# A fused attention and mixture-of-experts kernel on one core: last output tile in two halves, output stores of one batch reordered, and new order tables for all engines

## Chip, cores and metric

The kernel runs on one core of a Trainium2 chip. The metric is the device time in microseconds (us) of one execution; three runs of a kernel give a median. TensorE (PE) does the matmuls, VectorE (DVE), ScalarE (ACT) and GpSimd (POOL) the elementwise work, and SyncE (SP) only issues DMA transfers in this kernel.

## What is computed

Three stages in a row, all in 32-bit floats. Attention with a mask: every query and key goes to the nearest of 16 centroids, and a query sees only the keys of its own cluster. Its output, 1536 tokens of 512, goes through a layer `ln(solu(x @ w_in)) @ w_out` with 1024 inner columns, and then through `((x @ w_a) * (x @ w_b)) @ w_out` with 1536.

```python
q_assign = np.argmax(np.einsum('bhsd,hcd->bhsc', q_n, c_n), axis=-1)
mask = q_assign[:, :, :, None] == k_assign[:, :, None, :]
scores = np.where(mask, scale * np.matmul(q, k.transpose(0, 1, 3, 2)), -1000000000.0)
...
h = x @ w_in
solu = h * softmax(h)
x = (layernorm(solu) * g_ln) @ w_out
...
return (x @ w_a) * (x @ w_b) @ w_out
```

Shapes: 2 batches, 8 heads, 768 positions of 64; the output is two batches of 768 rows of 512 floats, twelve tiles of 128 rows and 256 KB.

## The kernel before

**A plan and order tables.** The program is first laid out as a list of operations. `Plan.add` (L245) takes one: its engine, a cost, a rank, and the buffers it reads and writes. Operations are numbered in the order in which they are added, and these numbers stand in the text below. `Plan.schedule` (L299) walks `SEQ` (from L37), one table of operation numbers for each engine, written into the file; each engine's instructions are issued strictly in the order of its table. What an operation depends on is worked out from its buffers, and an engine that comes to an operation whose inputs are not there waits, with all that stands behind it. The tables hold 840 entries for PE, 942 for DVE, 711 for ACT, 302 for POOL and 233 for SP. An operation can be several instructions: 12 matmuls, say.

**All transfers on one queue.** `dma` (L495) issues every DMA on SP, in the order of SP's table. A transfer whose source is not ready holds up those behind it.

**Precision by splitting.** A product of 32-bit floats is made of three matmuls of a rounded "hi" and a remainder "lo". So a weight or an activation takes an ACT cast (hi) and a subtraction on DVE (L485) or POOL (L483) for lo.

**The attention stage**, up to about 400 us, goes over eight pairs of heads. `do_load` (L669) loads q, k and v of a pair, 384 KB each. `qk_part` (L742) transposes and splits q and k; POOL's L758 and L760 make operands that `do_place` (L817) then copies from SBUF to SBUF into the layout that the scores need. `do_oh` (L922, ACT's L927) and `do_ohd` (L929) make the one-hot cluster rows and put them beside q and k, in transfers of 24 KB, four for each half of a pair. `score` (L1005) then has the score matmuls (L1014), the max (DVE L1018) and the exponential (ACT L1022); `turn` (L1030) transposes it (PE L1046, copies on ACT L1055 and DVE L1053); `apply` multiplies by v (PE L1070), merges halves (ACT L1083, DVE L1084) and normalises. Beside it run the weights of the next stage: `load_win` (L572) loads w_in and rounds and splits it with integer operations (DVE L579, POOL L595).

**The middle stage** is `moe_h`, `moe_ln`, `moe_x2` and `x_pack` (casts at L1294), up to about 400 us as well. **The last stage** works in 12 units; each has `quartet` (matmuls L1384, evacuations on ACT L1359, additions on DVE L1363 and L1369, hi on ACT L1373, lo on DVE L485) and then `moe2_y`, which multiplies a unit's 768 rows (six tiles of 128) by w_out (L1441). Two sums of a tile run in PSUM over the visits of a batch and are added on DVE (L1457) to a buffer in SBUF; after the last visit of a batch each tile's store to the output is issued (L1460). Batch 1 ends with unit 10, batch 0 with unit 11, the last. In unit 11 a tile gets three matmuls for each of two w_out blocks, 512 columns each. Tiles 0 and 1 are in the PSUM pair psS0, tiles 2 and 3 in psS1, tile 4 in psO, tile 5 in psM; psT0 and psT1 hold the quartet's results.

In this kernel tile 4 of unit 11 is added and stored in two halves of 256 columns, and the others whole; tile 0 is the last. SP's table ends with batch 1's six stores in the order of tiles 4, 2, 5, 3, 0, 1, and then batch 0's: 3, 5, 1, the halves of 4, 2, 0.

Of the kernel before, what the change touches and what calls it, by code (L numbers as in the profile page):

```python
# [83 lines left out]
    ),  # L84
    "DVE": (
# [287 lines left out]
def dve(n):  # L373
    return n / 0.96 + 69
# [1162 lines left out]
```

## Time and profile before

| | |
|---|---|
| median of 3 runs | 680.87 us (680.80 to 681.03) |
| profiled execution | 681.25 us |
| its span | 679.4 us |
| PE, DVE, ACT, POOL busy | 99%, 77%, 57%, 42% of the span |
| DMA | 58.49 MB moved, mean 86 GB/s |

The profile has one execution. Busy time is what instructions of an engine lasted; "idle before" is what an engine waited ahead of an instruction, with the engine or DMA that let it go. PE's weight loads (PEld) are recorded apart from its matmuls and overlap them. SPq is SP's queue of DMA issues. [...]

### The profile page before, as it was taken

To read this page: it belongs to the slowest core of one execution; us is meant where nothing else is said; L and a number is where in the kernel's file an instruction comes from. 1 tells how busy PE (TensorE), PEld (TensorE's weight loads), DVE (VectorE), ACT (ScalarE), POOL (GpSimd) and SP (SyncE) were. 2 spreads that over 40 slices of the span, in tenths; PEclk is the share of its full clock that TensorE was granted. 3 is DMA by queue.
4 is the path that set the end of the run, shared out by engine and by line. 5 is a ranking of instruction groups with operands and counts; after the bars stand their busy time and mean duration, and the time that the engine had idled before them with its cause. 6 is when DMAs were issued, how large, how long until landed. Compare 5 with 4: busy or idle time off the path is not lost.

```text
span 679.4 us, 10935 instructions
## 1 busy us (share of the span) xinstructions
PE 671.3 (99%) x3910; PEld 576.0 (85%) x3910; DVE 523.1 (77%) x943; ACT 389.4 (57%) x820; POOL 285.8 (42%) x323
## 2 busy tenths in 40 slices
PE   8999999999999999999999999999999999999997
PEld 7777777777777767888999999998989999989996
DVE  6978797798778878999869359796876757977436
ACT  5877777768677864574464555554654543534221
POOL 4024554635456433244445477644335432542000
PEclk9999999999999999999999999999999999999999
DMA  4367447473722612110211002132112212110005
GB/s 140 97 157 192 115 119 189 121 169 83 203 85 71 161 38 63 32 62 32 66 59 62 1 1 91 65 116 72 62 63 94 93 63 63 63 62 32 1 0 187
DMA packets 33094, 58.49 MB, mean 86 GB/s; under 512 B 3848, under 2 KB 21904, under 8 KB 33040
## 3 DMA queue, kind: packets, MB, share of 16 engines
q1 hardware_dynamic: 33040, 57.79, 30.0%
q8 instruction: 31, 0.51, 0.3%
q14 instruction: 23, 0.19, 0.1%
HBM read 36.74 MB, written 3.15 MB: 59 GB/s over the span
## 4 chain that ended last, share of the span: by engine, by line
PE 93%; DVE 4%; ACT 1%; DMA 1%; issue 1%; SPq 0%; DVEq 0%; ACTq 0%
PE psT L1384 25%; PE psS L1162 10%; PE psO L1070 10%; PE psS L1441 9%; PE psS L1014 9%; PE psT L1046 9%; PE psO L1254 5%; PE psM L1254 5%; PE psO L1441 2%; PE psM L1441 2%; PE psT L1237 2%; PE psM L750 1%; PE psM L841 1%; PE psM L1099 1%; PE psM L845 1%; DMA R<-R 1%
## 5 line engine op out<-in xcount | busy, mean ns | idle before, releaser
L1384 PE MATMUL psT<-R 128*128 128x384 f32 x1008 | 181.8, 336 | 0.4 <-DVE F L1363 0.3
L1384 PEld LDWEIGHTS psT<-R 128*128 128x128 f32 x1008 | 175.8, 188 | 4.8 <-ACT F L1359 1.3
L483 POOL TENSOR_TENSOR R<-F,R 128x256 fp32r<-128x256 f32 (+3 forms) x92 | 109.7, 1202 | 98.0 <-ACT R L1294 51.5
L595 POOL TENSOR_TENSOR F<-F 128x512 int32<-128x512 int32 x45 | 60.8, 1350 | 110.3 <-DVE F L591 96.3
L1359 ACT COPY F<-psT 128x384 f32<-128x384 f32 x108 | 51.5, 480 | 91.9 <-PE psT L1384 84.8
L1022 ACT ACTIVATE F<-psS,mxn 128x768 f32<-128x768 f32 x96 | 86.7, 905 | 23.2 <-DVE mxn L1018 16.7
L1018 DVE TENSOR_REDUCE mxn<-psS 128x1 f32<-128x768 f32 x96 | 90.4, 951 | 10.6 <-PE psS L1014 9.4
L1014 PE MATMUL psS<-R 128*128 128x512 f32 (+3 forms) x384 | 89.9, 358 | 0.9 <-DMA R<-R 0.6
L1046 PE MATMUL psT<-ident,F 128*128 128x128 f32 x576 | 85.8, 275 | 0.2
L1046 PEld LDWEIGHTS psT<-ident,F 128*128 128x128 f32 x576 | 65.4, 140 | 13.3 <-ACT F L1022 6.3
L1014 PEld LDWEIGHTS psS<-R 128*128 128x128 f32 (+1 forms) x384 | 65.6, 190 | 12.2 <-ACT F L1022 2.6
L1441 PE MATMUL psS<-R 128*128 128x512 f32 x288 | 74.9, 391 | 0.0
L1162 PE MATMUL psS<-R 128*128 128x512 f32 x288 | 69.3, 394 | 0.0
L1070 PE MATMUL psO<-F 128*64 128x384 f32 x384 | 69.0, 494 | 0.0
L1053 DVE COPY F<-psT 128x384 f32<-128x384 f32 x96 | 52.8, 550 | 15.5 <-PE psT L1046 14.2
L1441 PEld LDWEIGHTS psS<-R 128*128 128x128 f32 x288 | 53.8, 188 | 10.3
L1162 PEld LDWEIGHTS psS<-R 128*128 128x128 f32 x288 | 53.0, 188 | 10.5
L485 DVE TENSOR_TENSOR R<-F,R 128x384 fp32r<-128x384 f32 (+1 forms) x72 | 53.3, 753 | 8.5 <-ACT R L1373 3.9
L1363 DVE TENSOR_TENSOR F<-psT,F 128x384 f32<-128x384 f32 x48 | 26.7, 555 | 39.8 <-PE psT L1384 35.0
L1055 ACT COPY F<-psT 128x384 f32<-128x384 f32 x96 | 45.9, 479 | 19.7 <-PE psT L1046 18.3
L1369 DVE TENSOR_TENSOR F<-F 128x384 f32<-128x384 f32 x60 | 44.3, 742 | 10.6 <-ACT F L1359 10.1
L1070 PEld LDWEIGHTS psO<-F 128*64 128x64 f32 x384 | 24.7, 136 | 28.2 <-issue 26.6
(158 smaller groups left out, 1000.2 us busy)
## 6 DMA issues: line engine op xcount, KB each, us to landing
F<-in_moe_w_out_dram SPq DMA_DIRECT2D x20, 512.0 KB, 3.3
R<-R SPq DMA_DIRECT2D x28, 288.0 KB, 4.4
F<-in_moe_w_a_dram SPq DMA_DIRECT2D x12, 512.0 KB, 3.7
F<-in_moe_w_b_dram SPq DMA_DIRECT2D x12, 512.0 KB, 3.6
R<-R SPq DMA_DIRECT2D x28, 192.0 KB, 3.9
F<-in_moe_w_in_dram SPq DMA_DIRECT2D x8, 512.0 KB, 4.9
F<-in_v_dram SPq DMA_DIRECT2D x8, 384.0 KB, 5.1
out_dram<-F SPq DMA_DIRECT2D x11, 256.0 KB, 2.6
```

The source lines that it names most:

```text
L483: pl.add("POOL", pool(n), rank, lambda: G.tensor_tensor(out=out_, in0=in0, in1=in1, op=ALU.subtract), reads, writes)
L485: pl.add("DVE", dve(n), rank, lambda: V.tensor_tensor(out=out_, in0=in0, in1=in1, op=ALU.subtract), reads, writes, port=port)
L595: pl.add("POOL", pool(n), rank, lambda: G.tensor_tensor(out=ui, in0=ui, in1=low, op=ALU.add), [rk, lwk], [uk])
L1014: T.matmul(sp[:, c0:c0 + cn], kq[:r, 2 * m, t * P:(t + 1) * P], kq[:r, 2 * m + 1, c0:c0 + cn], start=m == 0, stop=m == 1)
L1018: pl.add("DVE", dve(S), i + SUB["max"], lambda: V.tensor_reduce(out=mxn[:, b:b + 1], in_=sp[:, :S], axis=AX.X, op=ALU.max, negate=True), [ ...
L1022: pl.add("ACT", act(S) + 93 + 93, i + SUB["exp"], lambda: A.activation(F[:, po:po + 768], sp[:, :S], AF.Exp, bias=mxn[:, b:b + 1], scale=1 ...
L1046: T.transpose(sp[:, c, :], pt[:, kt * P:(kt + 1) * P], ident)
L1070: T.matmul(psO[rs, :AN], vs[:, j, kt % HT * 2 + kt // HT], pt[:, kt, :], start=kt < 2, stop=kt >= NT - 2, tile_position=(0, kt % 2 * D), s ...
L1162: T.matmul(sp[:, n0:n0 + 512], xv5[:, i, a, c], winv[:, w, c, n0:n0 + 512], start=first, stop=(c == KD - 1 and a == 1))
L1254: T.matmul(sp[:, :GN], wo1v(f, w)[:, ds_], d[a][:, f, :], start=(f == 0 and x == 0), stop=(f == NF1 - 1 and x == 2))
L1384: T.matmul(t[:, :AN], wv[l][0][:, c], xp_[:, a, xi, c], start=(x in (0, 1, 3) and c == 0 and l == 0 and a == 0), stop=(c == 1 and l == 1), ...
L1441: T.matmul(yt, hy(j, a)[0][:, gg * P:(gg + 1) * P], R[:, wo + l * 512:wo + (l + 1) * 512], start=(u in first_u and fl == 0 and a == 0 and ...
```

## The change

Four things. First, all the order tables are replaced: 302 entries of PE's, 631 of DVE's, 432 of ACT's, 194 of POOL's and 178 of SP's stand at another place. Second, tile 0 of the last unit is taken out of `moe2_y` and done by a new function, `last_y`: two halves of 256 columns, in psT0 and psT1, each with all six matmuls (both w_out blocks), one addition and one store of 128 KB. All of it stands at the end of the tables. Third, tile 4's addition and store in two halves become one of each. Fourth, batch 1's stores stand on SP in the order of tiles 3, 5, 2, 4, 1, 0, which is the order in which DVE's table has their additions; batch 0's are 3, 5, 4, 1, 2 and the halves of 0.

The table entries that the prediction speaks of: 42, the v load of the first pair of heads; 142 and 141, place DMAs behind POOL's L758; 740 to 743 and 744 to 747, the one-hot DMAs of the first and the second half of pair 4; 732 and 701, place DMAs; 692, a v load; 713 and 317, w_in loads; 966, a rounding of w_in on DVE (L579); 1363, a merge on ACT (L1083); 1942, a cast on ACT (L1294); 2264, a subtraction on DVE (L485); 908, the k load of pair 6; 872, a v load; 929, a one-hot DMA.

```diff
     "SP": (
-        39, 7, 38, 107, 40, 41, 137, 187, 108, 42, 8, 142, 138, 139, 109, 158, 156, 165, 163, 166, 186, 164,
...
+        39, 7, 38, 40, 107, 41, 187, 138, 108, 8, 186, 142, 141, 42, 140, 139, 317, 153, 165, 163, 154, 158,
...
-        702, 732, 701, 692, 735, 688, 704, 731, 742, 740, 736, 700, 733, 713, 744, 743, 747, 746, 741, 918, 897,
...
+        703, 587, 734, 733, 704, 736, 705, 688, 732, 740, 741, 743, 742, 746, 692, 701, 747, 713, 744, 918, 897,
...
+        895, 916, 894, 896, 921, 917, 840, 919, 745, 899, 920, 898, 909, 923, 922, 925, 924, 929, 872, 908, 965,
...
-        2708, 2702, 2747, 2761, 2816, 2810, 2899, 2976, 2973, 2967, 2964, 2970, 2961, 3014, 3017, 3011, 3026,
-        3028, 3023, 3020,
...
+        2708, 2702, 2747, 2761, 2810, 2816, 2899, 2964, 2967, 2973, 2976, 2961, 2970, 3013, 3016, 3028, 3010,
+        3025, 3022, 3019,
     ),
...
+    def last_y(u, b):
+
+        o = ACC_[b * NT]
+        rk = T1 + (u + 2) * U
+        fj = [(fl, j) for j, (fl, half_) in enumerate(YO) if half_ == 0]
...
+        for x in range(2):
+            yt, yk, cs = psT[x][:, :DM // 2], f"psT{x}", slice(x * DM // 2, (x + 1) * DM // 2)
+            av, fk = F[:, o + cs.start:o + cs.stop], fc((o + cs.start, DM // 2))
+
+            def mm(yt=yt, cs=cs):
+                for fl, j in fj:
+                    for a, l in ((0, 0), (0, 1), (1, 0)):
+                        c0 = w0[fl] + l * 512 + cs.start
+                        T.matmul(yt, hy(j, a)[0][:, :P], R[:, c0:c0 + DM // 2], start=(fl == 0 and a == 0 and l == 0), stop=(fl == 1 and a == 1))
+
+            pl.add("PE", mm_cost(DM // 2, 6), rk + x * 0.6, mm, [*hk, *[rc((w, 1024)) for w in w0]], [yk])
+            pl.add("DVE", dve(DM // 2), rk + x * 0.6 + 0.1, lambda av=av, yt=yt: V.tensor_tensor(out=av, in0=yt, in1=av, op=ALU.add), [yk], [fk])
+            dma(128, rk + x * 0.6, lambda av=av, cs=cs: Y.dma_start(outv[b, 0, 0, :, cs], av), [fk], [])
...
+            if u == NU - 1 and t == 0:
+                if fl:
+                    last_y(u, b)
+                continue
...
-                m = 2 if u == NU - 1 and j == 3 and gg == 2 else 1
-                for x in range(m):
-                    cs = slice(x * DM // m, (x + 1) * DM // m)
-                    fk = fc((o + cs.start, DM // m))
-                    pl.add("DVE", dve(512 // m), rk + 0.1, lambda av=av[:, cs], yt=yt[:, cs]: V.tensor_tensor(
-                        out=av, in0=yt, in1=av, op=ALU.add), [yk], [fk])
-                    if not left[u]:
-                        dma(256 // m, rk, lambda av=av[:, cs], t=t, cs=cs: Y.dma_start(outv[b, t // HT, t % HT, :, cs], av), [fk], [])
+                fk = fc((o, 512))
+                pl.add("DVE", dve(512), rk + 0.1, lambda av=av, yt=yt: V.tensor_tensor(out=av, in0=yt, in1=av, op=ALU.add), [yk], [fk])
+                if not left[u]:
+                    dma(256, rk, lambda av=av, t=t: Y.dma_start(outv[b, t // HT, t % HT], av), [fk], [])
```

## Rows read from the trace of the kernel before

**Rows 1.** The page's chain of work that ended last: shares by engine.

```profile
PE 93%; DVE 4%; ACT 1%; DMA 1%; issue 1%; SPq 0%; DVEq 0%; ACTq 0%
```

**Rows 2.** Windows: length, busy PE, PEld, DVE, ACT, POOL, clock, DMA share, GB/s.

```profile
0.00:17.00 17.00, 14.56 (x91) 11.93 (x92) 11.86 (x31) 9.64 (x22) 7.77 (x35) 1.00 0.45 140
17.00:660.00 643.00, 641.33 (x3749) 550.95 (x3748) 500.09 (x894) 376.52 (x791) 278.05 (x288) 1.00 0.30 82
660.00:679.40 19.40, 15.38 (x74) 13.08 (x72) 11.18 (x20) 3.29 (x7) 0.00 (x0) 0.96 0.44 163
```

**Rows 3.** Timeline of the tail: start us, us, engine, line, what, count [idle before].

```profile
667.00 9.47 SPq L1460 DMA_DIRECT2D out_dram<-F  x13
...
673.86 1.52 PE L1441 MATMUL psS<-R 128*128 128x512 f32 x6
...
674.74 1.37 DVE L1457 TENSOR_TENSOR F<-psS,F 128x512 f32<-128x512 f32 x2
```

**Rows 4.** SP's last issue; DMA issues at 676.1 and 674.9: KB, us to landing.

```profile
676.14 0.33 SPq L1460 DMA_DIRECT2D out_dram<-F  x1
...
out_dram<-F SPq DMA_DIRECT2D x1, 256.0 KB, 2.0
...
out_dram<-F SPq DMA_DIRECT2D x1, 128.0 KB, 1.8
```

**Rows 5.** Groups by line and form: count | busy us, mean ns | idle before.

```profile
L1441 PE MATMUL psS<-R 128*128 128x512 f32 x288 | 74.9, 391 | 0.0
...
L1441 PEld LDWEIGHTS psS<-R 128*128 128x128 f32 x288 | 53.8, 188 | 10.3
...
L1014 PE MATMUL psS<-R 128*128 128x256 f32 x96 | 27.2, 283 | 0.0
...
L1457 DVE TENSOR_TENSOR F<-psO,F 128x256 f32<-128x256 f32 x2 | 0.8, 420 | 0.7 <-PE psO L1441 0.7
```

**Rows 6.** Timeline of PE in the opening.

```profile
8.79 0.83 PE L810 MATMUL psM<-cb,R 128*128 128x64 f32 x6
```

**Rows 7.** Timeline of PE near 133 us, and of SP from 123 us.

```profile
133.46 0.74 PE L1014 MATMUL psS<-R 80*128 80x512 f32 x3 [0.58 <-DMA R<-R]
...
123.31 1.20 SPq L934 DMA_DIRECT2D R<-R  x2
...
128.09 3.40 SPq L934 DMA_DIRECT2D R<-R  x5
```

**Rows 8.** Timeline of DVE and PE near 462 us.

```profile
460.06 2.23 DVE L485 TENSOR_TENSOR R<-F,R 128x384 fp32r<-128x384 f32 x2
462.21 0.54 DVE L1363 TENSOR_TENSOR F<-psT,F 128x384 f32<-128x384 f32 x1
...
462.81 0.62 PE L1384 MATMUL psT<-R 128*128 128x384 f32 x2 [0.25 <-DVE F L1363]
```

**Rows 9.** Timeline of PE's weight loads at three small waits.

```profile
179.80 0.31 PEld L1046 LDWEIGHTS psT<-ident,F 128*128 128x128 f32 x3 [0.80 <-ACT F L1022]
...
233.85 0.31 PEld L1046 LDWEIGHTS psT<-ident,F 128*128 128x128 f32 x3 [0.23 <-ACT F L1055]
...
402.88 0.47 PEld L1384 LDWEIGHTS psT<-R 128*128 128x128 f32 x3 [0.31 <-ACT F L1359]
```

**Rows 10.** DMA issues at 23.9 and 148 us; timeline of POOL, ACT and PE.

```profile
F<-in_v_dram SPq DMA_DIRECT2D x1, 384.0 KB, 5.5
...
F<-in_k_dram SPq DMA_DIRECT2D x1, 384.0 KB, 7.8
...
21.42 0.51 POOL L758 TENSOR_SCALAR R<-F 128x384 fp32r<-128x384 f32 x1 [6.56 <-ACT F L757]
...
27.80 2.16 PE L1070 MATMUL psO<-F 128*64 128x384 f32 x12
...
162.56 0.48 ACT L927 CAST R<-psM 128x384 fp32r<-128x384 bf16 x1
...
169.02 0.49 PE L750 MATMUL psM<-ident,F 128*128 128x128 f32 x3
```

More of the change, by code (lines that the diff above doesn't have):

```diff
@@ L1428, in tile_cluster_attention_moe_moe2 @@
     left = {us[-1]: sum(1 for b2, v in visits[i + 1:] if b2 == b) for i, (b, us) in enumerate(visits)}
+    def last_y(u, b):
+        o = ACC_[b * NT]
+        rk = T1 + (u + 2) * U
+        fj = [(fl, j) for j, (fl, half_) in enumerate(YO) if half_ == 0]
+        hk = [rc((HY_ + j * 2 * AN, P), (HY_ + (j * 2 + 1) * AN, P)) for fl, j in fj]
+        w0 = [WY_[(u // 2 * 2 + fl) % 3] for fl in range(2)]
+        for x in range(2):
[9 more added lines that the diff above has]
+            dma(128, rk + x * 0.6, lambda av=av, cs=cs: Y.dma_start(outv[b, 0, 0, :, cs], av), [fk], [])
     def moe2_y(u, j):
```

315 rows, old and new, of the table SEQ are left out of this document.

## Prediction, made before the change was run

> **What bounds the kernel now.** I read four views: the chain of work that ended last (who is on it), the windows (where TensorE, PE, is idle), the timeline round each idle place (what it waited for), and the DMA issues of the same moments. The chain is PE for 93%, VectorE (DVE) for 4% [rows 1]. In three windows PE is busy 14.56 of 17, 641.33 of 643 and 15.38 of 19.4 us [rows 2]. The reader is to see three places where time can be saved: the opening, some 1.7 us of idle in the long middle, and the tail, where 4 us pass after the last matmul. The middle's idle understates what a wait costs: matmuls are pipelined, a 512-column one lasts 391 ns while six take 1.52 [rows 3, 5], so they start every (1.52 − 0.39)/5 = 0.226 us; a matmul that comes late loses the shown idle plus that overlap, 0.391 − 0.226 = 0.16. Sums are made against the profiled execution, 681.25 us with a span of 679.4; the median is 680.87, and I carry the difference over to it.
>
> **Tail: the last tile in two halves.** Now the last three matmuls of tile 0 end at 673.86 + 1.52 = 675.38, a 512-column addition of 1.37/2 = 0.69 follows, and the last store is issued at 676.14 [rows 3, 4]. It is 256 KB and lands after 2.0; a 128 KB store nearby took 1.8 [rows 4]. After the change the last addition has 256 columns, 0.42 each now [rows 5]: −0.27. The last store has 128 KB: −0.2. PE pays for it. A 256-column matmul lasts 283, a 512-column one 391 [rows 5], so columns cost 108 ns per 256, and 256-column ones should start every 0.226 − 0.108 = 0.118 us: twelve take 1.42 where six took 6 × 0.226 = 1.36: +0.06. The weight loads double in number (12 for 6) and run beside the matmuls. Three of tile 0's six old matmuls came early, and now all twelve stand at the end; that moves other tiles' matmuls earlier by the same time and costs nothing by itself. Tail: −0.27 − 0.2 + 0.06 = about **−0.4**; bounds −0.55 and +0.43. The upper one is for weight loads that set the pace, 188 ns each in L1441 [rows 5]: 12 × 0.188 − 1.36 = +0.90 for PE, so −0.27 − 0.2 + 0.90. I take the lower price because six L810 matmuls of 64 columns, each with a load of its own, take 0.83 together [rows 6], so one in at most 0.14; the rest of their price is in the range.
>
> The trace lets the halves start about twice as often as the wholes. [...]
>
> **Order of batch 1's stores, and tile 4's two halves made whole.** The 13 stores leave from 667.00 on, after waiting for tile 4's addition, all while PE has work to 675.38 [rows 3]. The last one follows its addition within 0.03 us (676.11 to 676.14) [rows 3, 4], so SP's queue had drained. Sending the first six earlier gains nothing: **0**, and up to +0.2 if it brings more traffic under batch 0's. Tile 4's single addition of 0.69 for 0.84 in two parts: 0, hidden by PE.
>
> **Tables, 133 us.** PE's score matmul waited, idle 0.58, for an SBUF-to-SBUF DMA [rows 7]: the one-hot rows 741 and 743 of pair 4's first half. On SP they stand behind w_in load 713 and among the five of the row at 128.09, after the second half's 744; each such issue takes 1.20/2 = 0.6 [rows 7]. The change puts 740, 741, 743, 742 together, directly behind 732 and ahead of 713, 744, 746 and 747, so they leave from about 123.3 and land, even after 4 us, before 128.3, five before they are read. What is passed over (713, 746, 747, 692 and 701) has no reader as near. What is late next is PE itself. 0.58 plus an overlap of 0.16 to 0.24: **−0.8**.
>
> **462 us.** PE's idle of 0.25 waits for DVE's L1363 [rows 8]: it began at 462.21, behind two L485 subtractions (460.06, 2.23 us), though the matmuls it reads were done before. In the new DVE table 2264 (one of these, 1.1) and a 0.55 operation go behind L1363, three of 0.41 to 0.43 come ahead: about −0.45, so the wait is gone: 0.25 + 0.16 = **−0.4**. The moved subtraction ends later; its reader is on PE some microseconds on.
>
> **Three small ones.** PE's weight load for the transposes at 179.80 waits 0.80 for an exponential [rows 9], that one for a max reduction, and that stood behind a DVE w_in operation (966), which goes behind it; PE's matmuls themselves start about 0.2 late: −0.2. At 233.85 PE waits for an ACT copy that stood behind L1083's (1363), 0.23 for the weight load; at 402.88 its weight load waits 0.31 for an evacuation that stood behind a cast (1942) [rows 9]. Both go behind: −0.2 and −0.25. A move of one engine's operation past another issues nothing else; none of these has a DMA. Together **−0.65**.
>
> **The opening** is reordered on DVE and ACT too. I find no wait that it surely removes: **0**, bounds −0.15 and +0.15.
>
> **What the new order can spoil.** Some thousand entries change place, POOL's among them, and a wait it makes is in no row of this trace. I bound it by nothing and by the middle's whole present idle, 1.67 [rows 2], and take **+0.5**, a third of that, since the moves that I followed mostly leave PE's order as it was.
>
> The sum: −0.4 + 0 − 0.8 − 0.4 − 0.65 + 0 + 0.5 = −1.75, that is 679.5 for the profiled execution and **679.1** beside the median. The terms' ends give 677.9 (tail −0.55, opening −0.15, no new wait, half a microsecond of idle gone that I didn't trace) to 679.6 (new waits of 1.0).
>
> **Rivals.** *Waits change place.* The one-hot DMA, the subtraction and the cast that moved back now come late elsewhere, as many as were removed, and only the tail's gain stays: 680.87 − 0.4 = 680.4, with 680.9 where the tail gives nothing either. For it: PE is already 99.7% busy in the middle [rows 2], so any operation on another engine that comes 0.2 late shows. Against: the 133 us wait is the largest and its DMAs get some five microseconds of room.
>
> *Halves dear on PE.* If starts and not columns set the pace, twelve halves cost up to 0.9 more than six wholes, since a weight load lasts 188 ns [rows 5]; half of that is 0.45. The tail is then 0 to +0.43, and with the rest kept the time is 679.5 to 679.9. For it: the last matmuls run with nothing else beside them. Against: the L810 row, where loads overlap. [...]
>
> *Slower: big loads put back too far.* On SP the first v load (384 KB, before issued at 13.59) goes behind two place DMAs that wait for POOL's L758, over at 21.42 + 0.51 [rows 10]: two issues later, about 23.2, it leaves (behind it on SP wait two more place DMAs and w_in load 317, with later readers), and PE first reads it at 27.80 (about 28.9 after, where two more PE operations stand ahead). The k load 908 goes behind a one-hot DMA that waits for ACT's L927 (162.56; about 162.0 after) and a v load: 163.3, and PE's L750 needs it at 169.02 [rows 10]. A v load at about that time took 5.5, the slowest 384 KB load 7.8 [rows 10]. It decides where a load takes over 5.7. At 5.5 both are in time, the first by 0.2 only; at 7.8 the first is 23.2 + 7.8 − 28.9 = 2.1 late, the second 163.3 + 7.8 − 169.0 = 2.1: +4.2 − 1.75, so 683.3. Against it: the 7.8 came with far more DMA work queued than stands before either.
>
> **Chances.** Forecast 0.57; waits change place 0.27; halves dear 0.07; slower 0.09. A measurement of this kernel can tell about 0.2% (1.36 us) from no change, so faster is below 679.51 and slower above 682.23. The forecast's range 677.9 to 679.6 lies nearly all below the first bound; halves dear is split. Faster 0.59, same 0.32, slower 0.09. The range takes in the forecast and nearly all of the second case, and leaves out the slower one and some 0.1 more: 677.9 to 680.8.
>
> **What would show it.** In the new trace: a last L1457 addition of 256 columns (0.42) followed by a 128 KB store landing in 1.8, and the end some 4 − 0.47 = 3.6 after the last matmul; twelve last matmuls in about 1.4 us; no wait of L1014 on a DMA near 133; no L1363 wait near 462; the idle of 17 to 660 below 1.0. I am wrong if that idle is as large as before at other places (second case), if PE's last twelve matmuls take over 1.8 (third), or if L1070 near 28 or L750 near 169 waits for a DMA of v or k (fourth).

## The result: slower by 0.7%

| | before | after |
|---|---|---|
| median | 680.97 us (6 runs) | 685.90 us (6 runs) |
| ratio | | 1.0067 (95% interval 1.0054 to 1.0080) |
| span of the profiled execution | 679.4 us | 684.2 us |

The forecast was 679.1, range 677.9 to 680.8. The tail and the wait at 133 us came out about as priced. The loss lies where the prediction had put a zero, in the opening; in new waits, whose sum it had taken too low; and in small moves whose gain did not last. The windows of the kernel after, with the columns of [rows 2]:

```profile
0.00:17.00 17.00, 13.14 (x79) 9.92 (x79) 11.67 (x27) 8.79 (x19) 7.65 (x35) 0.94 0.42 121
17.00:660.00 643.00, 640.64 (x3735) 550.15 (x3735) 502.12 (x891) 376.48 (x793) 276.51 (x288) 1.00 0.30 83
660.00:684.20 24.20, 21.02 (x105) 18.28 (x103) 14.21 (x25) 4.16 (x9) 0.00 (x0) 0.99 0.36 131
...
14.00:16.00 2.00, 0.66 (x4) 0.50 (x4) 1.97 (x4) 0.10 (x1) 1.07 (x2) 0.74 0.89 275
16.00:18.00 2.00, 2.00 (x8) 1.30 (x9) 0.84 (x2) 1.26 (x3) 0.00 (x0) 0.50 0.89 292
18.00:20.00 2.00, 2.00 (x9) 1.81 (x9) 1.05 (x3) 0.25 (x2) 0.00 (x0) 0.50 0.20 67
20.00:22.00 2.00, 2.00 (x8) 1.93 (x8) 1.58 (x3) 0.27 (x1) 0.00 (x0) 0.56 0.00 0
22.00:24.00 2.00, 1.66 (x11) 1.27 (x11) 1.51 (x3) 1.62 (x4) 0.00 (x0) 1.00 0.00 0
```

Look at the column after POOL's, PE's granted clock as a share of the full one. In before it is 1.00 in both windows up to 660 us; here it falls to 0.50 between 16 and 20 us. PE is busy only 0.66 of the 2 us from 14 to 16. After that it is busy all the time, yet with only 8 or 9 matmuls in 2 us: the six of L810 take 1.32 at 17.57, where in before they take 0.75 at 15.35. The window from 17 to 660 has 643.00 - 640.64 = 2.36 us of idle PE, where the prediction wanted to see less than 1.0.

To find where the rest went I set the start of the n-th PE operation of the kernel after against the n-th of before. The difference is -0.1 at 10 us, +4.0 at 18, +3.8 at 35 (0.24 won back by a better order of two transposes and an exponential), +4.0 at 120, +3.0 at 140 (the wait at 133 is gone: -0.85 from 130 on), +3.2 at 310, +4.4 at 340, +4.7 at 410, +5.9 at 430 and +5.6 at 670; after the last matmul it falls to +4.8. Each kernel has one trace; that such differences also move by some tenths between two executions is an estimate, from the times of the kernel before, 680.6 to 683.3 us.

**The opening.** Timeline near 13 us, first of the kernel before (two lines), then of the kernel after:

```profile
12.93 0.59 DVE L888 TENSOR_TENSOR F<-F,mx 128x192 bf16<-128x192 f32 x1
13.57 0.35 PE L905 MATMUL psM<-F 128*64 128x128 bf16 x3
...
12.65 0.50 POOL L793 TENSOR_SCALAR R<-R 64x384 fp32r<-64x384 f32 x1
12.78 2.50 DVE L888 TENSOR_TENSOR F<-F,mx 128x192 bf16<-128x192 f32 x1
13.12 1.94 POOL L760 TENSOR_TENSOR R<-F,R 128x384 fp32r<-128x384 f32 x2
...
15.34 0.53 PE L905 MATMUL psM<-F 128*64 128x128 bf16 x3 [1.39 <-DVE F L888]
```

In the kernel after, DVE's L888 begins while POOL works and ends at 15.28, just after POOL's third operation in a row (13.12 + 1.94 = 15.06). At 25.12, with POOL idle, the same operation takes 0.35. PE waits 1.39 for it, and then its clock is at 0.50.

**The new waits in the middle** look alike. At 425 and at 309, DVE beside POOL:

```profile
425.03 1.31 POOL L595 TENSOR_TENSOR F<-F 128x512 int32<-128x512 int32 x1 [1.50 <-DVE F L591]
425.05 1.71 DVE L1369 TENSOR_TENSOR F<-F 128x384 f32<-128x384 f32 x1 [0.17 <-ACT F L1359]
426.68 0.54 DVE L1363 TENSOR_TENSOR F<-psT,F 128x384 f32<-128x384 f32 x1
427.28 0.97 PE L1384 MATMUL psT<-R 128*128 128x384 f32 x4 [0.70 <-DVE F L1363]
...
308.98 1.31 DVE L1199 SCALAR_TENSOR_TENSOR stt<-stt 128x1 f32<-128x1 f32 x1
...
309.00 1.28 POOL L483 TENSOR_TENSOR R<-F,R 128x512 fp32r<-128x512 f32 x1 [0.73 <-ACT R L612]
```

An L1369 takes 0.55 alone and an L1199 0.22. Here neither ends before the POOL operation beside it: L1199 ends with it (310.29 and 310.28), L1369 0.42 later (426.76 and 426.34). Below, a DVE operation that takes longer beside a running POOL operation than without one is called held.

**The tail** is as the prediction had it. Timeline of the end, to be read against [rows 3, 4]:

```profile
679.43 1.59 PE L1445 MATMUL psT<-R 128*128 128x256 f32 x12
680.34 0.42 DVE L1448 TENSOR_TENSOR F<-psT,F 128x256 f32<-128x256 f32 x1
680.80 1.05 SPq L1449 DMA_DIRECT2D out_dram<-F  x2
681.06 0.42 DVE L1448 TENSOR_TENSOR F<-psT,F 128x256 f32<-128x256 f32 x1 [0.29 <-PE psT L1445]
```

The last matmul ends at 679.43 + 1.59 = 681.02 and the span at 684.17: 3.15 where before had 4.04. Of this gain of 0.89, 0.30 lies behind the landing of the last store and isn't the new tail's (see the end).

### The profile page after: what moved, and what is told of

It is laid out like the page before. It is cut to its first block, busy times and chain, and to the rows that moved or that the text cites. A ratio compares the mean times of both kernels' runs of the same rounds, so it can differ in the third digit from the quotient of the medians.

```text
span 684.2 us, 10970 instructions
## 1 busy us (share of the span) xinstructions
PE 674.8 (99%) x3916; PEld 578.4 (85%) x3916; DVE 528.0 (77%) x943; ACT 389.4 (57%) x820; POOL 284.2 (42%) x323
## 3 DMA queue, kind: packets, MB, share of 16 engines
HBM read 36.74 MB, written 3.15 MB: 58 GB/s over the span
## 4 chain that ended last, share of the span: by engine, by line
PE 91%; DVE 6%; ACT 1%; issue 1%; DMA 0%; POOL 0%; DVEq 0%; ACTq 0%
PE psT L1384 24%; PE psS L1014 10%; PE psT L1046 9%; PE psO L1070 9%; PE psS L1466 9%; PE psS L1162 8%; PE psM L1254 5%; PE psO L1254 5%; PE psO L1466 2%; PE psM L1466 2%; PE psM L841 2%; PE psT L1237 1%; PE psM L750 1%; DVE F L1369 1%; PE psM L1099 1%
## 5 line engine op out<-in xcount | busy, mean ns | idle before, releaser
L483 POOL TENSOR_TENSOR R<-F,R 128x512 fp32r<-128x512 f32 (+3 forms) x92 | 109.2, 1196 | 110.0 <-ACT R L1294 58.6
L595 POOL TENSOR_TENSOR F<-F 128x512 int32<-128x512 int32 x45 | 61.2, 1363 | 100.4 <-DVE F L591 90.5
L1022 ACT ACTIVATE F<-psS,mxn 128x768 f32<-128x768 f32 x96 | 86.7, 904 | 23.9 <-DVE mxn L1018 17.4
L1070 PE MATMUL psO<-F 128*64 128x384 f32 x384 | 69.0, 495 | 0.0
L485 DVE TENSOR_TENSOR R<-F,R 128x384 fp32r<-128x384 f32 (+1 forms) x72 | 57.1, 810 | 11.6 <-ACT R L1373 6.7
L1363 DVE TENSOR_TENSOR F<-psT,F 128x384 f32<-128x384 f32 x48 | 26.6, 555 | 36.6 <-PE psT L1384 27.1
L1369 DVE TENSOR_TENSOR F<-F 128x384 f32<-128x384 f32 x60 | 41.9, 708 | 10.4 <-ACT F L1359 10.0
L1070 PEld LDWEIGHTS psO<-F 128*64 128x64 f32 x384 | 24.7, 136 | 28.2 <-issue 26.5
```

What stands on the lines that cost most here:

```text
L483: pl.add("POOL", pool(n), rank, lambda: G.tensor_tensor(out=out_, in0=in0, in1=in1, op=ALU.subtract), reads, writes)
L485: pl.add("DVE", dve(n), rank, lambda: V.tensor_tensor(out=out_, in0=in0, in1=in1, op=ALU.subtract), reads, writes, port=port)
L595: pl.add("POOL", pool(n), rank, lambda: G.tensor_tensor(out=ui, in0=ui, in1=low, op=ALU.add), [rk, lwk], [uk])
L1022: pl.add("ACT", act(S) + 93 + 93, i + SUB["exp"], lambda: A.activation(F[:, po:po + 768], sp[:, :S], AF.Exp, bias=mxn[:, b:b + 1], scale=1 ...
L1070: T.matmul(psO[rs, :AN], vs[:, j, kt % HT * 2 + kt // HT], pt[:, kt, :], start=kt < 2, stop=kt >= NT - 2, tile_position=(0, kt % 2 * D), s ...
```

## Experiments

In the comparisons below the kernel before ran beside each on the same chip and took 681.4 to 681.7 us, so ratios are compared. All but the run with work added for PE and those with the new tail change entries of the tables alone.

**POOL's opening put back.**

```diff
     "POOL": (
-        2, 6, 0, 10, 4, 77, 5, 45, 81, 112, 116, 49, 117, 113, 132, 133,
+        2, 6, 4, 0, 10, 5, 49, 77, 112, 81, 113, 116, 117, 45, 132, 133,
```

> The kernel after, with the first 14 entries of POOL's table in the order of the kernel before; nothing else. Theory P (three POOL operations run back to back at 12.65 to 15.06, DVE's L888 is held beside them for 2.5 us instead of about 0.6, PE waits 1.4 for it and its granted clock falls to the lower level until 22): L888 lasts 0.6 or less, no low clock in 14 to 22, time 685.9 - 4.0 = 681.9, give or take 0.4. Theory W (the warm-up matmuls that moved on PE let the clock fall): the clock still falls, 685 to 686. Theory S (the many new waits later make it slower): 685.5 or more.

Measured: ratio 1.0002 (0.9992 to 1.0011), 681.92 us; the clock is 1.00 throughout. Timeline of this run:

```profile
12.71 0.51 POOL L758 TENSOR_SCALAR R<-F 128x384 fp32r<-128x384 f32 x1
12.83 0.60 DVE L888 TENSOR_TENSOR F<-F,mx 128x192 bf16<-128x192 f32 x1
13.30 1.01 POOL L760 TENSOR_TENSOR R<-F,R 128x384 fp32r<-128x384 f32 x1
13.46 0.90 DVE L890 TENSOR_SCALAR F<-F 128x96 bf16<-128x96 bf16 x1
13.92 0.36 PE L905 MATMUL psM<-F 128*64 128x128 bf16 x3
```

POOL pauses between 13.22 and 13.30, and L888 takes 0.60 and not 2.50: it ends at 13.43. Fourteen entries of POOL's table hold nearly the whole loss. With them put back the change is neither faster nor slower than before: the forecast's 1.75 us is still missing.

**POOL's opening of after in the kernel before.**

```diff
     "POOL": (
-        2, 6, 4, 0, 10, 5, 49, 77, 112, 81, 113, 116, 117, 45, 132, 133,
+        2, 6, 0, 10, 4, 77, 5, 45, 81, 112, 116, 49, 117, 113, 132, 133,
```

> The kernel before, with the first 14 entries of POOL's table in the order of the kernel after; nothing else. Theory P: L888 lasts about 2.5, PE waits about 1.4 near 14 us and the clock falls: 681.0 + 4.0 = 685.0. Theories W and S: no change, 680.8 to 681.3.

Measured: 686.27 us, ratio 1.0073 (1.0058 to 1.0088). The timeline and the clock of two windows:

```profile
12.98 2.49 DVE L888 TENSOR_TENSOR F<-F,mx 128x192 bf16<-128x192 f32 x1
13.32 1.94 POOL L760 TENSOR_TENSOR R<-F,R 128x384 fp32r<-128x384 f32 x2
15.53 0.49 PE L905 MATMUL psM<-F 128*64 128x128 bf16 x3 [1.93 <-DVE F L888]
...
16.00:18.00 2.00, 2.00 (x7) 1.30 (x7) 0.88 (x3) 0.76 (x2) 0.00 (x0) 0.50 0.99 368
18.00:20.00 2.00, 2.00 (x9) 1.80 (x9) 0.78 (x2) 0.75 (x3) 0.00 (x0) 0.50 0.04 9
```

So POOL's order alone is enough, in either direction.

**The wait kept, PE given work in it.** The kernel after with

```diff
-            pl.add("PE", 227, 1e6 + 100 + x, lambda: T.matmul(psS[1][:, :512], cb[:, :P], cb[:, :512], start=True, stop=True), ["cb"], ["psS1"], release=WARM[0])
+            pl.add("PE", 227, 1e6 + 100 + x, lambda x=x: [T.matmul(psS[1][:, :512], cb[:, :P], cb[:, :512], start=True, stop=True) for _ in range(7 if x == 5 else 1)], ["cb"], ["psS1"], release=WARM[0])
```

> The kernel after, in which the sixth warm-up operation issues seven matmuls instead of one, so that PE has 1.4 us of work while it waits for L888 (the added matmuls write a PSUM bank that nobody reads). If most of the loss is the lower clock and not the wait itself: L888 still lasts 2.5, the clock stays at its upper level, 685.9 - 2.5 = 683.4. If the wait itself is the loss: 685.5 to 686.

Measured: 684.01 us, ratio 1.0035 (1.0023 to 1.0046).

```profile
12.92 2.52 DVE L888 TENSOR_TENSOR F<-F,mx 128x192 bf16<-128x192 f32 x1
13.37 2.07 PE L732 MATMUL psS<-cb 128*128 128x512 f32 x8
15.49 0.35 PE L905 MATMUL psM<-F 128*64 128x128 bf16 x3
...
14.00:16.00 2.00, 1.95 (x11) 1.23 (x9) 1.97 (x3) 0.12 (x1) 1.22 (x2) 1.00 0.76 255
16.00:18.00 2.00, 2.00 (x13) 1.48 (x13) 1.45 (x4) 1.49 (x4) 0.00 (x0) 1.00 0.89 272
```

L888 is as long as ever (2.52), yet with PE given work beside it the clock stays at 1.00, where in the kernel after, with PE idle for 1.39, it is at 0.50. By the ratios the fall costs 1.0067 - 1.0035 = 0.0032 of 681.6, or 2.2 us. By the n-th PE operation, the added ones left out, this run stands at +1.6 at 18 us and the kernel after at +4.0: 2.4 for the clock there, and 1.6 for the late L888 itself. I had expected 2.5 for the clock.

**PE's order round the warm-up matmuls, in the kernel before.**

```diff
     "PE": (
-        121, 122, 87, 91, 72, 123, 69, 124, 125,
+        121, 87, 91, 122, 123, 72, 124, 69, 125,
```

> The kernel before, with only the nine PE entries round the warm-up matmuls (121 to 125) in the order of the kernel after. Theory P: within 0.4 of 681.0, the clock stays up. Theory W: the clock falls near 14 us, 683.5 to 685.

Measured: ratio 1.0004 (0.9994 to 1.0013), clock 1.00. The moved warm-up matmuls are not the cause.

**The one-hot DMAs alone, in the kernel before.**

```diff
     "SP": (
-        742, 740, 736, 700, 733, 713, 744, 743, 747, 746, 741,
+        742, 740, 743, 741, 736, 700, 733, 713, 744, 747, 746,
```

> The kernel before, with only two SP entries moved: the one-hot DMAs 741 and 743 directly behind 740. Theory (the wait at 133 us is what the queue order cost, 0.58 idle plus overlap): no wait on a DMA near 133, ratio to before 0.9988 (-0.8 us). Rival (the wait takes another place, as the sum's forecast rival had it): ratio 1.0000.

Measured: ratio 0.9987 (0.9978 to 0.9995), -0.9 us. Timelines of PE and SP:

```profile
133.00 0.97 PE L1014 MATMUL psS<-R 128*128 128x512 f32 x4
...
123.93 2.46 SPq L934 DMA_DIRECT2D R<-R  x4
```

The four one-hot DMAs leave together at 123.93 and the score matmuls run through [rows 7]. Against before the PE starts step forward by 0.85 at 133 us (+0.62 to -0.23) and keep that to the end: this gain is not given back.

**The tail alone, in the kernel before**: `last_y` and its entries, all other entries in the old order (the numbers of the last tiles' operations shift with the new function).

```diff
     "PE": (
-        3004, 3008, 3007, 3003, 3012, 3006, 3015, 3009, 3005, 3024, 3021, 3018,
+        3003, 3007, 3006, 3011, 3005, 3014, 3008, 3004, 3026, 3023, 3020, 3017,
```

> The kernel before, with only the tail changed: tile 0 of the last unit in two halves of 256 columns, tile 4 whole, all else in the order of before (the stores of batch 1 too). Theory: -0.4 to -0.8 us, ratio 0.999, the twelve last matmuls in about 1.4 us. Rival (starts and not columns set the pace of 256-column matmuls): twelve last matmuls 1.8 to 2.3 us, ratio 1.000 to 1.0006.

Measured: ratio 0.9998 (0.9989 to 1.0006), which tells neither. Its trace does: the same twelve matmuls in 1.59, as in the kernel after, so they start every (1.59 - 0.28)/11 = 0.119 us, and from the last matmul to the end 3.60 instead of 4.04. The rival of dear halves is out. A likely reason why the time shows so little of it is in the section on the hardware.

**Batch 1's store order alone, in the kernel before.**

```diff
     "SP": (
-        2899, 2976, 2973, 2967, 2964, 2970, 2961,
+        2899, 2964, 2967, 2973, 2976, 2961, 2970,
```

> The kernel before, with only batch 1's six stores in the new order on SP (tiles 3, 5, 2, 4, 1, 0). Theory (they lie under PE's work and SP's queue has drained before the last store): ratio 1.0000, the last store issued 0.03 us after its addition as before. Rival (later batch 1 stores collide with batch 0's, or the earlier start clears the way): 0.2 to 0.4 us either way, ratio 0.9995 or 1.0005.

Measured: ratio 1.0006 (0.9997 to 1.0015), no difference that can be told. From the last matmul to the end its trace has 4.04, as before.

**The priced moves and nothing else, in the kernel before**: tail, one-hot DMAs, and

```diff
 ACT:  1942 behind 2067;  1363 behind 1357
 DVE:  966 behind 1042;  2264, 2194, 2272, 2190  ->  2264, 2190, 2272, 2194
```

> The kernel before with the moves that the prediction priced and nothing else: tail, one-hot DMAs, ACT's 1942 behind 2067 and 1363 behind 1357, DVE's 966 behind 1042, and near 462 DVE's 2190 and 2272 ahead of 2194. If the priced terms are right and the loss lies in what the full tables add: -0.4 -0.8 -0.25 -0.2 -0.2 -0.4 = -2.25 to -2.6, ratio 0.9964. If each removed wait is given back: ratio 0.999 to 1.000.

Measured: ratio 0.9989 (0.9980 to 0.9998), no more than the one-hot DMAs alone. Timeline at two of the moves:

```profile
179.37 0.55 PE L1046 MATMUL psT<-ident,F 128*128 128x128 f32 x3
...
180.13 0.94 PE L841 MATMUL psM<-R,cb 128*128 128x384 f32 x4 [0.21 <-DVE F L851]
...
236.16 0.76 PEld L1014 LDWEIGHTS psS<-R 128*128 128x128 f32 x4 [0.23 <-ACT F L1022]
```

The wait at 179.80 is gone, its transposes come 0.19 earlier against the n-th operation of before, and the next thing on PE then waits for DVE's L851: nothing is left, and 0.26 of the one-hot gain goes with it. The ACT copy at 233.85 gives 0.24, all given back at 236.16; the evacuation at 402.88 gives 0.26, all given back at 407.4. Near 462, 0.26 comes of the 0.4, and the operations that follow don't take it back. (From 490 to 660 us this trace loses 0.17 in small steps; the tail-only run, without these moves, loses 0.28 there, so it isn't they that do it.)

**Two holds of the middle undone**, in the kernel after with POOL's opening put back.

```diff
 POOL:  1682, 1540, 1601, 1639  ->  1682, 1601, 1540, 1639
 DVE:   2033, 2096, 2101, 2106  ->  2033, 2101, 2096, 2106
```

> The kernel after with POOL's opening as in the kernel before, and two more entries moved: POOL's subtraction 1540 behind 1601 (so that DVE's small L1199 near 314 us runs with POOL idle) and DVE's L1363 (2101) ahead of the L1369 (2096) that POOL's L595 holds near 421 us. Theory P (the new waits in the middle are DVE operations held beside a running POOL operation): L1199 0.22 instead of 0.98, PE's waits at 311 to 320 and at 422.7 gone, -0.75 -0.85: ratio to before 0.998. Rival (these waits come from other moves): ratio 1.000, as without the two.

Measured: ratio 0.9981 (0.9972 to 0.9990), 680.40 us. DVE and POOL at 420:

```profile
420.38 1.32 POOL L595 TENSOR_TENSOR F<-F 128x512 int32<-128x512 int32 x1 [1.49 <-DVE F L591]
420.94 0.56 DVE L1363 TENSOR_TENSOR F<-psT,F 128x384 f32<-128x384 f32 x1 [0.72 <-PE psT L1384]
421.42 0.69 DVE L1369 TENSOR_TENSOR F<-F 128x384 f32<-128x384 f32 x1
```

L1363, which reads PSUM and only one operand from SBUF, lasts 0.56 beside POOL's L595 of 1.32, so isn't held, and the step of 0.85 that stood on PE behind it is gone. The L1369 behind it takes 0.69, where in the kernel after it took 1.71. At 314 the L1199 is back to 0.22, and half of the step there is gone (0.45 of 0.88).

**A third hold undone**: the kernel of the last run with

```diff
 DVE:  1660, 1676, 1661, 1662  ->  1660, 1661, 1662, 1676
```

> The run with two holds undone and one more edit: DVE's L1199 and L1201 (1661, 1662) ahead of the L1185 (1676), so that L1199 near 305 us starts before POOL's L483 does. Theory P: L1199 there 0.22 instead of 1.31, PE's late start at 311.8 (0.45) gone; time 680.4 - 0.45 in that measure, ratio to before 0.9974. Rival (the L1199 is late for another reason, or the wait moves on): ratio 0.998 as without it.

Measured: ratio 0.9977 (0.9969 to 0.9986), 679.72 us; less than either kernel takes. Minimum, median and maximum of L1199 in the kernel after and in this one:

```profile
L1199 DVE SCALAR_TENSOR_TENSOR stt<-stt x12: 199/220/1315, 272.1 to 381.0; 128x1 f32<-128x1 f32 x12
```

```profile
L1199 DVE SCALAR_TENSOR_TENSOR stt<-stt x12: 202/220/302, 268.3 to 375.8; 128x1 f32<-128x1 f32 x12
```

The step of 0.45 at 312 is gone from its PE starts. The interval overlaps that of the run before it, so the last 0.0004 rest on the trace.

**The terms that lasted, in the kernel before**: tail, one-hot DMAs, the DVE moves near 462, and after's order on PE, ACT and DVE from 23 to 33 us (exponential 201 ahead of the copies 105 and 106). Part of that order:

```diff
 PE:   206, 202, 204, 220, 213, 211  ->  204, 202, 206, 211, 213, 220
 ACT:  198, 106, 105, 205, 201, 208, 225, 212  ->  198, 201, 205, 105, 106, 208, 212, 225
```

> The kernel before with the two priced terms that lasted (one-hot DMAs, tail in halves), the two DVE moves near 462, and the order of the kernel after on PE, ACT and DVE between 23 and 33 us, where the run with POOL's opening restored had gained 0.3. If terms that lasted add up: -0.85 -0.4 -0.25 -0.3 = -1.8, ratio 0.9974. If the 23 to 33 us order is given back later: ratio 0.9978.

Measured: ratio 0.9977 (0.9969 to 0.9986), 679.98 us. By the PE starts the order from 23 to 33 us gives 0.24 and keeps it; at the last matmul they are 1.25 further ahead of before than at 18 us. Of the tail's gain this one trace shows nothing: its last store took 2.3 us to land instead of 1.7, and from the last matmul to the end it has 4.05.

## Why the prediction was wrong

**The opening (0, bounds ±0.15) failed**, by some 4 us. The step asked which wait the new DVE and ACT orders remove and never followed POOL's fourteen entries. It took the durations of DVE operations for fixed. They were not fixed in the trace of before either: near 462 two L485 took 2.23 us [rows 8], where one lasts 0.54 at the least, and POOL's L483 (1.55 from 459.28) and L585 (0.84 from 460.91) ran beside them; I moved such operations about and priced them by the length they happened to have. The runs show which ones: DVE operations that were held read two operands from SBUF (shortest and longest of one form in the kernel after: L888 0.35 and 2.50, L1369 0.54 and 1.71, L1199 0.20 and 1.31, L485 0.54 and 1.67) or one in some forms (L890, 0.18 at 25.85 in the kernel after and 0.90 in the run with POOL's opening put back), and L1363 with one operand in PSUM lasts 542 to 559 ns in all its 48 instances of the kernel after, 24 of which began while POOL was at work. One and the same subtraction, L485, shows the difference (minimum, median and maximum in ns, kernel after): with both operands in SBUF the longest took 1924, with one in PSUM 694, though nine of those 24 began while POOL was at work. Why it is so, the records don't tell.

```profile
L485 DVE TENSOR_TENSOR R<-F,R x72: 542/559/1924, 354.8 to 676.2; 128x384 fp32r<-128x384 f32 x48, 128x512 fp32r<-128x512 f32 x24
L485 DVE TENSOR_TENSOR R<-psT,R x24: 635/682/694, 282.2 to 385.1; 128x512 fp32r<-128x512 f32 x24
```

**The clock** was in no term of the sum. PE's idle place of 1.39 us, with the clock at 0.50 behind it, cost 2.2 to 2.4 beyond itself (the run with PE given work, where it stays at 1.00).

**The allowance for new waits (+0.5, bound 1.67) failed** too: with POOL's opening put back the change still stands at +1.2 us before the tail by the n-th PE operation, where the priced terms alone should have it at about -1.85: a gap of some 3 us. About 0.8 of it, by the run with the priced moves, are small moves that did not last (next paragraph); the other 2.2 are new waits, where the sum had 0.5 and the bound 1.67. The bound was wrong in kind. A wait that doesn't exist yet isn't limited by the idle time that there is. Three of these waits are shown to be holds of DVE beside POOL, worth 0.9 at 422, 0.45 for the L1199 at 314 and 0.45 for the one at 305 (times of the run with POOL's opening put back; about 4 us later in the kernel after); the others, some 0.4 together, weren't tried one by one.

**The small moves (-0.65, and -0.4 near 462) were mis-read**: the waits went, as forecast, and 0.19 to 0.26 came with each, but three of four were given back within 0.8 to 5 us, since the engine that had been late was late again at its next operation. Of -1.05 some -0.26 lasted. I had named what is late next only for the 133 us wait. The rival "waits change place" was right on this point.

**What held.** The 133 us wait: -0.8 priced, -0.9 measured, kept to the end. The halves: 0.118 us priced for a start, 0.119 found; the last addition 0.42; the last store, 128 KB, landed 1.7 us after its issue. From the last matmul to the end, where 0.47 was priced, the tail won 0.44 in the run with it alone and 0.56 in that with the priced moves; it won nothing in the last run above, whose store landed late. The store order: 0. The large loads: L1070 and L750 did not wait for v or k in the kernel after, so the slower rival didn't come; the time is slower by another mechanism, which none of the rivals named. (By its own terms the low end of the range is 677.8, not 677.9; nothing hangs on that.)

## To carry to other kernels

Here the length of a DVE operation went with what POOL did at that moment (L888 0.60 or 2.50 us, L1199 0.22 or 1.31): before a move is priced, look for operations of one form whose lengths differ by a factor of two or more, and lay the other engine's timeline beside them. Look first at the places where such a stretch would leave PE idle: here the clock's fall behind one idle stretch of 1.39 us cost more (2.2 to 2.4) than the late operation itself (1.6). And of four small waits that were removed here three gave back their 0.19 to 0.26 within 0.8 to 5 us: follow the chain past the next two or three operations of the engine that was late.

## What the hardware showed that was not expected

**A DVE operation was held over several POOL operations, not one.** L888 lasted 2.50 us beside three POOL operations back to back (12.65 to 15.06), and 0.60 where POOL paused for 0.08 us (12.83 + 0.60 = 13.43 in the run with POOL's opening put back).

**POOL's operations were long beside DVE too, and not in every trace.** In the profiled execution of the tail-only run POOL's L483 near 447 took 3.18 us, beside a row of DVE operations, and PE waited 0.90 for it; in the one of before it took 1.34, and DVE's L1369 beside it 1.66 and not 0.55. First two lines of before, then the tail-only run:

```profile
446.70 1.34 POOL L483 TENSOR_TENSOR R<-F,R 128x512 fp32r<-128x512 f32 x1 [2.82 <-ACT R L1294]
446.80 1.66 DVE L1369 TENSOR_TENSOR F<-F 128x384 f32<-128x384 f32 x1
...
446.58 0.68 DVE L485 TENSOR_TENSOR R<-F,R 128x512 fp32r<-128x512 f32 x1
447.18 0.55 DVE L1369 TENSOR_TENSOR F<-F 128x384 f32<-128x384 f32 x1
447.64 1.16 DVE L485 TENSOR_TENSOR R<-F,R 128x512 fp32r<-128x512 f32 x2
...
447.08 3.18 POOL L483 TENSOR_TENSOR R<-F,R 128x512 fp32r<-128x512 f32 x1 [2.83 <-ACT R L1294]
...
450.32 3.94 PE L1384 MATMUL psT<-R 128*128 128x384 f32 x21 [0.90 <-POOL R L483]
```

Its PE starts fall back by 1.15 there against before, of which 0.9 lasts, and the same step stands in the trace of the run with after's POOL opening in the kernel before. The tables are the same at that place, and these operations start at the same distances from each other in both traces, to 0.02 us; what decides which of the two is the long one isn't in the records. Each kernel has one trace, so it isn't shown that executions of one kernel differ in this way. If they do, it is one source of the spread of 680.6 to 683.3 us among executions of the kernel before; with that spread 0.4 us of the tail can't be read from the times.

**Open.** From the landing of the last store to the end the kernel before has 1.24 us and the kernel after 0.95. The new tail isn't the cause: with it and before's other tables (the tail alone, the priced moves, the terms that lasted) it is 1.24 to 1.25, as in all runs made from the kernel before, and 0.94 to 0.95 in all runs made from the kernel after. In the records of the queues the difference lies in a pause among POOL's last semaphore instructions: 0.33 us in the kernel before, 0.04 in the kernel after. What decides it was not tried.
